# A layer with linear attention and a feed-forward branch on one core: chunks of 58 numbers laid out 64 apart

## The chip, the core and the metric

The kernel runs on one core of a Trainium2 chip. The core has five engines with instruction queues of their own: PE (TensorE, the matrix engine; its weight loads are listed as PEld), DVE (VectorE), ACT (ScalarE), POOL (GpSimd) and SP (SyncE, which here only issues DMAs). They meet through semaphores. Data lies in SBUF, matmul results in PSUM, which has eight banks of 512 fp32 numbers per partition. The metric is the device time of one execution in microseconds (us), taken as the median of several runs; beside it there is one profiled execution with a trace.

## The reference

One input x of 2048 tokens by 448 is normalised over its rows (layer norm), and two branches are added to it:

```python
def _A_ref(x, wqkv, w_phi, wo):                      # H = 16 heads, Dh = 28
    qkv = (x @ wqkv).reshape(B, S, 3, H, Dh) ...
    pq = einsum("bhsd,hdf->bhsf", q, w_phi)          # pk the same from k
    phi_q = concatenate([softmax(pq), softmax(-pq)], axis=-1)   # phi_k the same
    kv  = einsum("bhsf,bhsd->bhfd", phi_k, v)
    z   = einsum("bhsf->bhf", phi_k)
    num = einsum("bhqf,bhfd->bhqd", phi_q, kv)
    den = einsum("bhqf,bhf->bhq", phi_q, z)[..., None] + 1e-6
    return (num / den).transpose(...).reshape(B, S, D) @ wo

def _B_ref(x, w1, w2):                               # F = 1792
    return silu(x @ w1) @ w2

xn = _layernorm(x)
return x + _A_ref(xn, wqkv, w_phi, wo) + _B_ref(xn, w1, w2)
```

All inputs and the output are bf16. The attention is linear: kv and z are sums over all tokens, and no product of tokens with tokens is made.

## The kernel before

The 2048 tokens are 16 tiles of 128, mostly handled as pairs of tiles. The kernel first records operations (`P.op`, `P.dma`) with their reads and writes; a planner (`schedule`, L228) then gives every engine its order from estimated durations. For PE the order is fixed beforehand: the words of `PLAN` (L361) are taken one after the other and chained by `strict`. For the other engines the planner decides.

A word of `PLAN` has a phase, a kind, a number and, after `@`, the PSUM banks that it opens. The kinds: `F` is a block of the first feed-forward product (two column groups of 128 for 512 tokens), `v`, `k` and `q` are the projections of a pair of tiles, `K` is the kv product of two tiles, `M` joins and masks kv, `s` scales the query features of a pair, `U` is the attention product of a pair, `G` and `Y` are seven steps of the second feed-forward product of a pair, `W` is the output projection of a pair, `E` are the last feed-forward steps of the last two tiles. A product over 128 rows is made as two products over 64 rows that run side by side on the two halves of the matrix engine. Phase `a` has tile 0 of the pair on the lower and tile 1 on the upper rows, phase `b` the other way round, so each phase is half of the work of a block (`rows64`, L903). A half may begin only when the partner half that wrote the same bank from the other rows is done, and for that PE waits for its own semaphore.

The stretches that the change touches:

- `v_block` (L789) projects the values. Its evacuation (ACT, L542) writes them into `vaug` (L461), where each head has 28 values and a 1 (`DA` = 29); the ones give z. The ones are written by a clear on POOL (L1054).
- `kv` (L852) multiplies, for each tile and each chunk c of two heads, 128 columns of key features with the 58 numbers of the chunk, on both row halves. The results of a half gather in one bank, chunk c at columns 58c. These are 256 matmuls in 16 blocks of 8 chunks.
- `kvm` (L883): ACT copies one half out of PSUM, DVE adds the other (`kvsum`), and DVE multiplies by a mask that zeroes the cross terms of the two heads (`KVm`, L466, cleared on POOL, L1055).
- `att` (L956) multiplies the query features of a tile (stationary, in `phT`) with `KVm`, chunk by chunk, again 58 columns at 58c of a bank: 256 matmuls in 16 blocks.
- `normalise` (L967), after phase `b`: on DVE it adds epsilon to the denominators, takes the reciprocal and multiplies, into `o_sb`; SP issues one transposing DMA per tile (`dma_t`, L623) into `oT_sb`, which `wo_pair` (L984) reads. `o_sb` and `oT_sb` lie in the same memory as `vaug`, which is no longer needed then.
- After the last part of a pair, `finish_pair` (L1010) adds the other addend on DVE (L1001) and ACT issues the output DMA (L1003).

The query features come from `phi_q` (POOL, L874), behind the row sums (DVE, L837) and reciprocals (L838) of the exponents that ACT makes, and go through transposing DMAs on SP as well.

Before the change a chunk of the values starts at element 58c of its tile's row of 464 bf16 numbers, so at byte 116c, and a chunk of results at byte 232c of its bank.

Of the kernel before, what the change touches and what calls it, by code (L numbers as in the profile page):

```python
# [6 lines left out]
BF16 = mybir.dt.bfloat16  # L7
F32 = mybir.dt.float32
# [355 lines left out]
aF23@2 bF21 ak14@6 bF23 bY0 g0@1 bk14 bY0 aF13@0 aF19@2 bF13 aF24@6 aF20@4 bF19 bF20 bF24 ak10@0 g1@3 bk10 K0 K6 K4 aq4@2  # L364
K12 aq8@4 bq4 K8 K2 s4 aq0@0 bq8 aq6@2 K14 bq0 bq6 bY1@45 K10 M aY1 aq2@2 aF26@0 s6 bq2 bF26 bY1 aG3@23 aY1 aU2@67 s8 aF15@0
bU2 s0 bF15 aF16@4 bG3 bF16 aU4@01 aq12@6 bU4 bq12 aU3@45 bG3 bU3 s2 aq10@0 aG3 bq10 aq14@6 aW2@45 aG2 s10 bq14 aU0@01 bG2
bG2 aG4@67 bU0 bW4 bW2 bG4 s12 aG2 aW3 s14 aU1@01 bW3 aG4 aW4 bU1 bG4 bG5@23 aG6@41 aU5@50 aU6@67 bU5 aG5 bG6 aU7@05 bG6 bU6
aG6 bG5 bU7 aG5 aW0@67 bW5 bW0 aW5 aW6 aW1@05 aG7@672 aW7 bW6 bW1 bG7 bW7 E14 E15"""


def bass_parallel_sum__linear_kernel_hedgehog__dense_activation_silu__prompt_kernel(
# [19 lines left out]
    KS = (0, 128, 256, D - 128)  # L391
    CC = 8
    DA = DH + 1
    EPS_LN = 1e-5
    EPS_DEN = 1e-6
    NYT = 4
# [11 lines left out]
    with es:  # L408
        def sb(name, shape, dt):
            return es.enter_context(nc.sbuf_tensor(name, shape, dt))  # L410
# [32 lines left out]
        def ph_slots(n, w=1):  # L443
            at = n * CC * 128 + (SHIFT if n >= NT - 2 else 0)
            return flat[:, at:at + w * CC * 128].rearrange("p (t c j) -> p t c j", t=w, c=CC)
# [12 lines left out]
            c = t % 2 * EW  # L458
            return ek_pairs(t - t % 2, t - t % 2 + 2)[:, 0, c:c + w * EW].rearrange("p (n c) -> p n c", n=w)

        vaug = sb("vaug", [128, NT, H, DA], BF16)  # L461
        vflat = vaug[:].rearrange("p t h e -> p (t h e)")
        o_sb = vflat[:, 0:NO * 512].rearrange("p (n c) -> p n c", n=NO)
        oT_sb = vflat[:, NO * 512:(NO + NQ) * 512].rearrange("p (n g c) -> p n g c", n=NQ, g=G)
        kvsum = sb("kvsum", [KP, CC * 2 * DA], F32)
        KVm = sb("KVm", [128, CC, 2, DA], BF16)  # L466
        ident = sb("ident", [128, 128], BF16)
        ones_bf = sb("ones_bf", [128, 128], BF16)
        ones4 = sb("ones4", [128, 4], F32)
# [45 lines left out]
        def pe_mms(mms, name, dur=None, keys_w=(), mode=128):  # L515
            def fn(e):
                r = None
                for dst, lhsT, rhs, st, sp in mms:
                    r = e.matmul(dst, lhsT, rhs, start=st, stop=sp, skip_group_check=True)  # L519
# [28 lines left out]
        def memset(dst, v, n, name, eng="pool"):  # L548
            P.op(eng, d_pool(n, 0.5), lambda e: e.memset(dst, v), writes=[dst], name=name)  # L549
# [239 lines left out]
        def v_block(t, b0):  # L789
            fns = pair_block(b0, D, lambda i, kt, r: xnT[r, t + i, kt, :],  # L790
                             lambda i, kt, r: wv_sb[r, kt, :], "v")

            def evac():
                src = psum[:, b0 * 512:(b0 + 2) * 512].rearrange("p (i c) -> p i c", i=2)[:, :, 0:D].rearrange("p i (h d) -> p i h d", h=H)
                dst = vaug[:, t:t + 2, :, 0:DH]
                act(dst, src, ACTF.Identity, 896, f"v_ev{t}")

            return *fns, evac
# [53 lines left out]
        def kv(ts):  # L852
            def rows_k(t, c, r):
                at = t % 2 * EW + c * KP
                return ek_pairs(t - t % 2, t - t % 2 + 2)[r, 0, at:at + 128]

            P.cur_slack = 250.0
            pe_mms([(banks[KVB - i][:, c * 2 * DA:(c + 1) * 2 * DA], rows_k(t, c, r),
                     vaug[r, t, 2 * c:2 * c + 2, :].rearrange("p h c -> p (h c)"),
                     t == 0 and c == 0, t == NT - 1) for t in ts for c in range(CC) for i, r in enumerate((LOW, HIGH))],  # L860
                   "kv_mm", dur=CC * 29.0 * len(ts), keys_w=["kvbank"], mode=64)
            P.cur_slack = 0.0

        def slot(t):
            n = q_order.index(t)
            return n + 14 if n < 2 else n + 6 if n < 8 else n - 8
# [14 lines left out]
                      (1250.0, 2450.0)[w - 1], "phqT", (1250.0, 2000.0)[w - 1])  # L881

        def kvm():  # L883
            lo, hi = (banks[KVB - i][0:KP, 0:2 * DA * CC] for i in range(2))
            P.op("act", d_act(464), lambda e: e.activation(kvsum[:], hi, ACTF.Identity), reads=[hi], writes=[kvsum[:]], name="kvhi")
            P.op("dve", d_dve(464), lambda e: e.tensor_tensor(kvsum[:], lo, kvsum[:], ALU.add), reads=[lo, kvsum[:]], writes=[kvsum[:]], name="kvsum")
            src = kvsum[:].rearrange("p (c j e) -> p c j e", c=CC, j=2)
            P.op("dve", d_dve(464), lambda e: e.tensor_tensor(
                KVm[0:KP], src, mask2[:, None, :, None].broadcast_to([KP, CC, 2, DA]), ALU.mult),
                reads=[src, mask2[:]], writes=[KVm[0:KP]], name="kvm")  # L890


        early = {int(w[2]) for w in PLAN.split() if w[1:2] == "Y"}
# [62 lines left out]
        def att(p, turned, bs):  # L956
            both = []
            for side in range(2):
                i = side ^ turned
                both.append([(bs[i], slice(c * 2 * DA, (c + 1) * 2 * DA), ph_slots(slot(2 * p + i))[LO_HI[side], 0, c, :],  # L960
                              KVm[LO_HI[side], c, :, :].rearrange("p j e -> p (j e)")) for c in range(CC)])
            rows64(*both, "U_mm", CC * 31.2, 400.0, turned)
            if turned:
                for i in range(2):
                    normalise(2 * p + i, banks[bs[i]])

        def normalise(t, ub):  # L967
# [4 lines left out]
            U3 = ub[:, 0:H * DA].rearrange("p (h e) -> p h e", e=DA)  # L972
            P.op("dve", 190, lambda e: e.tensor_scalar(den[:, uq, :], U3[:, :, DH], EPS_DEN, None, ALU.add),
                 reads=[U3[:, :, DH]], writes=[den[:, uq, :]], name="den")
# [4 lines left out]
            o3 = o_sb[:, oq, off:off + D].rearrange("p (h d) -> p h d", d=DH)  # L979
            P.op("dve", 620, lambda e: e.tensor_tensor(o3, U3[:, :, 0:DH], rden[:, uq, :, None].broadcast_to([128, H, DH]), ALU.mult),  # L980
                 reads=[U3[:, :, 0:DH], rden[:, uq, :]], writes=[o3], name="o")
            dma_t(oT_sb[:, q, :, :], o_sb[:, oq, :], 620.0, "oT_dma")

        def wo_pair(p, turned, bs, last):  # L984
# [66 lines left out]
            ln_tile(t)  # L1051
        chain("ev3 bnst4".split())
        block_mask(mask2[:], 2 * DH, 2, KP)
        memset(vaug[:, :, :, DH], 1.0, 2150, "vaug1")  # L1054
        memset(KVm[:], 0.0, 464, "kvm0")  # L1055
        def k_block(t, b0):
            return proj_block(t, b0, True)

# [199 lines left out]
```

## Time and profile before

| | us |
|---|---|
| median of 3 runs | 145.98 |
| lowest and highest | 145.75, 146.19 |
| the profiled execution | 145.67 |
| its span, first to last instruction | 144.4 |
| PE busy in the span | 140.5 |
| DVE, ACT, POOL busy | 90.4, 79.7, 75.1 |

The page of the profile gives busy times per engine, the chain of work that ended last, and groups of instructions; further views are the timeline (instructions in order of time, equal ones merged: start, length, engine, line, operation, tiles, shape, count, and in brackets the idle time before it and who ended it), the view by tile, and windows (busy time per engine in a stretch). Every matmul is listed as `PE ... MATMUL` with "64*128 64x58" for 64 rows, 128 stationary columns and 58 moving columns. Matmuls are pipelined, so their listed durations overlap; the distance of the starts is the cost of a step. The mean granted clock of PE over the span is 1.00.

### The profile page before, as it was taken

The page shows a single profiled execution, that of the slowest core. Times are in us where ns is not written, and L with a number is a line of the kernel's source. Part 1 is how long each engine was busy: PE and PEld are TensorE (multiplying, and loading weights), DVE is VectorE, ACT ScalarE, POOL GpSimd, SP SyncE. Part 2 cuts the span into 40 slices and gives each one's busy share as a digit, 9 for nine tenths or more (in the row PEclk, how much of TensorE's full clock was granted, in tenths as well). Part 3 has the DMA queues.
Part 4 walks back from the last instruction along what each step waited for, and adds up shares of the span by engine and source line. Part 5 has one row for each costly group of instructions (what it writes and reads, how often), then busy time and mean ns, then how long its engine had stood idle before and what let it go on. Part 6 is the DMA issues. An engine that isn't in the chain of part 4 may idle for free.

```text
span 144.4 us, 4551 instructions
## 1 busy us (share of the span) xinstructions
PE 140.5 (97%) x1966; PEld 82.6 (57%) x1966; DVE 90.4 (63%) x195; ACT 79.7 (55%) x98; POOL 75.1 (52%) x95
## 2 busy tenths in 40 slices
PE   7799999999999999999999999999999999999994
PEld 7694445445444545476677655565555556555773
DVE  1969898700850079939049999957886564265163
ACT  4578775479996999889878948265440000000000
POOL 8807668620296009799935999991596500000000
DMA  3999989847960000000000068759689899524432
GB/s 90 330 346 299 278 180 91 155 88 166 354 182 5 0 2 5 0 0 5 0 5 5 5 124 161 120 108 184 97 166 164 203 197 181 108 53 97 130 127 64
DMA packets 44500, 17.59 MB, mean 122 GB/s; under 512 B 36912, under 2 KB 44096, under 8 KB 44480
## 3 DMA queue, kind: packets, MB, share of 16 engines
q1 hardware_dynamic: 41776, 15.22, 51.9%
q10 hardware_dynamic: 2576, 2.06, 5.4%
q8 instruction: 15, 0.25, 0.7%
q0 software_dynamic: 128, 0.03, 0.1%
q14 instruction: 5, 0.04, 0.1%
HBM read 6.57 MB, written 1.84 MB: 58 GB/s over the span
## 4 chain that ended last, share of the span: by engine, by line
PE 94%; DVE 2%; DMA 1%; issue 0%
PE psum L519 94%; DMA x_sb<-in_A_x_dram 1%; DVE st L701 1%; DVE RA L716 1%; PE psum L536 1%; DVE mv L702 0%; DVE x_sb L1001 0%; DVE rstd L707 0%
## 5 line engine op out<-in xcount | busy, mean ns | idle before, releaser
L519 PE MATMUL psum<-xnT,phT 64*128 64x512 bf16 (+1 forms) x428 | 46.8, 350 | 0.1
L519 PE MATMUL psum<-w_sb,hT 64*128 64x448 bf16 (+4 forms) x455 | 46.0, 341 | 0.0
L837 DVE TENSOR_REDUCE Rec<-Ek_sb 128x32 f32<-128x896 bf16 (+1 forms) x20 | 24.6, 1257 | 18.7 <-ACT Ek_sb L542 18.6
L542 ACT ACTIVATE hT<-psum 128x1024 bf16<-128x1024 f32 x28 | 27.6, 1024 | 11.0 <-PE psum L519 11.0
L519 PEld LDWEIGHTS psum<-w_sb,hT 64*128 64x128 bf16 (+1 forms) x455 | 23.6, 94 | 17.4 <-issue 0.2
L519 PEld LDWEIGHTS psum<-xnT,phT 64*128 64x128 bf16 (+1 forms) x428 | 22.5, 95 | 17.9 <-ACT vaug L542 0.6
L874 POOL TENSOR_TENSOR RA<-Ek_sb,Rec 128x896 bf16<-128x896 bf16 x16 | 27.0, 1721 | 5.8 <-DVE Rec L838 4.7
L519 PE MATMUL psum<-Wqk,xnT 64*128 64x432 bf16 x224 | 24.6, 343 | 0.0
L542 ACT ACTIVATE Ek_sb<-psum 128x864 bf16<-128x864 f32 x24 | 20.4, 915 | 7.2 <-PE psum L519 2.9
L847 POOL TENSOR_TENSOR Ek_sb<-Ek_sb,Rec 128x896 bf16<-128x896 bf16 x8 | 13.4, 1697 | 17.7 <-DVE Rec L838 17.7
L519 PEld LDWEIGHTS psum<-Wqk,xnT 64*128 64x128 bf16 x224 | 10.9, 94 | 8.1 <-ACT hT L542 0.4
L542 ACT ACT_TABLE_LOAD x11 | 14.1, 1283 | 2.1 <-POOL Wp L549 1.9
L847 POOL TENSOR_TENSOR phT<-phT,Rec 128x896 bf16<-128x896 bf16 x8 | 13.4, 1697 | 1.6 <-issue 0.9
L519 PE MATMUL psum<-wv,xnT 64*128 64x448 bf16 x112 | 12.4, 349 | 0.0
L1001 DVE TENSOR_TENSOR x_sb<-psum,x_sb 128x448 bf16<-128x448 f32 (+2 forms) x13 | 7.2, 584 | 7.5 <-PE psum L519 7.4
L701 DVE BATCH_NORM_STATS2 st<-x_sb 128x6 f32<-128x448 bf16 x16 | 9.7, 603 | 3.4 <-DMA x_sb<-in_A_x_dram 3.4
L519 PE MATMUL psum<-wo_sb,vaug 64*128 64x448 bf16 (+2 forms) x102 | 11.1, 338 | 0.1
L716 DVE TENSOR_SCALAR RA<-x_sb,mv,rstd 128x384 bf16<-128x384 bf16 (+4 forms) x29 | 9.1, 352 | 1.3 <-POOL rstd L712 1.2
L980 DVE TENSOR_TENSOR vaug<-psum,rden 128x448 bf16<-128x448 f32 x16 | 9.3, 620 | 0.0
L837 DVE TENSOR_REDUCE Rec<-phT 128x64 f32<-128x1792 bf16 x4 | 8.0, 1991 | 1.8 <-ACT phT L542 1.8
L838 DVE RECIPROCAL Rec<-Rec 128x32 f32<-128x32 f32 (+1 forms) x24 | 8.8, 396 | 0.2
L542 ACT ACTIVATE vaug<-psum 128x896 bf16<-128x896 f32 x8 | 7.3, 929 | 2.4 <-PE psum L519 2.4
(60 smaller groups left out, 106.3 us busy)
## 6 DMA issues: line engine op xcount, KB each, us to landing
out_dram<-x_sb ACTq DMA_DIRECT2D x15, 112.0 KB, 2.0
w_sb<-in_B_w_dram SPq DMA_DIRECT2D x1, 1568.0 KB, 7.8
x_sb<-in_A_x_dram SPq DMA_DIRECT2D x3, 448.0 KB, 6.3
wo_sb<-in_A_wo_dram SPq DMA_DIRECT2D x2, 336.0 KB, 7.4
phT<-in_B_w_dram SPq DMA_DIRECT2D x1, 576.0 KB, 7.4
phT<-in_B_w_dram SPq DMA_DIRECT2D x1, 384.0 KB, 5.1
wv<-in_A_wqkv_dram SPq DMA_DIRECT2D x1, 336.0 KB, 7.6
phT<-in_B_w_dram ACTq DMA_DIRECT2D x1, 256.0 KB, 4.6
```

What stands on the lines that cost most here:

```text
L519: r = e.matmul(dst, lhsT, rhs, start=st, stop=sp, skip_group_check=True)
L536: r = e.transpose(dst, src, ident[:])
L542: P.op("act", d_act(n), lambda e: e.activation(dst, src, func, scale=scale), reads=[src], writes=[dst], table=table, name=name, **keys)
L701: P.op("dve", 590, lambda e: e.bn_stats(st6[:, t, :], xs), reads=[xs], writes=[st6[:, t, :]], name=f"bnst{t}", okeys_w=["ln"])
L716: P.op("dve", dur, lambda e: e.tensor_scalar(dst, x_sb[:, t, c0:c1], mv[:, t, 0:1], rstd[:, t:t + 1], ALU.subtract, ALU.mult), reads=[xs, ...
L837: P.op("dve", 50 + 967 * n, lambda e: e.tensor_reduce(R2, E4, AXL.X, ALU.add), reads=[E4], writes=[R2], name=f"Ssum_{tag}")
L838: P.op("dve", 135 + 210 * n, lambda e: e.reciprocal(R2, R2), reads=[R2], writes=[R2], name="Rrec")
L847: P.op("pool", 1700, lambda e: e.tensor_tensor(E3, E3, Rk[:, :, None].broadcast_to([128, 32, DH]), ALU.mult), reads=[E3, Rk], writes=[E3], ...
L874: P.op("pool", 1700, lambda e: e.tensor_tensor(dst, Eq, Rq.rearrange("p (c j) -> p c j", c=CC)[:, :, :, None].broadcast_to([128, CC, 4, DH ...
L980: P.op("dve", 620, lambda e: e.tensor_tensor(o3, U3[:, :, 0:DH], rden[:, uq, :, None].broadcast_to([128, H, DH]), ALU.mult), reads=[U3[:, ...
L1001: P.op("dve", d_dve(cs.stop - cs.start), lambda e: e.tensor_tensor(res[:, cs], ob, addend[:, cs], ALU.add), reads=[ob, addend[:, cs]], wri ...
```

## The change

Values, masked kv and the results of both products get a pitch of 64 numbers per chunk (`CP`), of which the first 58 (`CW`) are used. The order of PE changes in three places: `K12` goes ahead of `aq4`, `bG5` ahead of `aG6`, and `bW6` ahead of `aG7` and `aW7`. The number of matmuls and their columns stay as they are. The planner's costs of the two products are set to other values. As the planner orders them, nothing but these three places changes on PE; SP, ACT and DVE keep their order, and on POOL four of eight small clears after the first kv products change places.

```diff
-aF23@2 ... ak10@0 g1@3 bk10 K0 K6 K4 aq4@2
-K12 aq8@4 bq4 K8 K2 s4 ...
+aF23@2 ... ak10@0 g1@3 bk10 K0 K6 K4 K12
+aq4@2 aq8@4 bq4 K8 K2 s4 ...
-... aU7@05 bG6 bU6
-aG6 bG5 bU7 aG5 aW0@67 bW5 bW0 aW5 aW6 aW1@05 aG7@672 aW7 bW6 bW1 bG7 bW7 E14 E15
+aU7@05 bG6 bU6 bG5 aG6 bU7 aG5 aW0@67 bW5 bW0 aW5 aW6 aW1@05 bW6 aG7@672 aW7 bW1 bG7 bW7 E14 E15
...
+    CW, CP = 2 * DA, 64
...
-        vaug = sb("vaug", [128, NT, H, DA], BF16)
-        vflat = vaug[:].rearrange("p t h e -> p (t h e)")
+        vaug = sb("vaug", [128, NT, CC, CP], BF16)
+        vflat = vaug[:].rearrange("p t c x -> p (t c x)")
+
+        def by_head(ap):
+            return ap[:, :, 0:CW].rearrange("p c (j e) -> p c j e", j=2)
...
-        kvsum = sb("kvsum", [KP, CC * 2 * DA], F32)
-        KVm = sb("KVm", [128, CC, 2, DA], BF16)
+        kvsum = sb("kvsum", [KP, CC, CW], F32)
+        KVm = sb("KVm", [128, CC, CP], BF16)
...
-                dst = vaug[:, t:t + 2, :, 0:DH]
+                dst = vaug[:, t:t + 2, :, 0:CW].rearrange("p i c (j e) -> p i c j e", j=2)[:, :, :, :, 0:DH]
...
-            pe_mms([(banks[KVB - i][:, c * 2 * DA:(c + 1) * 2 * DA], rows_k(t, c, r),
-                     vaug[r, t, 2 * c:2 * c + 2, :].rearrange("p h c -> p (h c)"),
+            pe_mms([(banks[KVB - i][:, c * CP:c * CP + CW], rows_k(t, c, r),
+                     vaug[r, t, c, 0:CW],
                      t == 0 and c == 0, t == NT - 1) for t in ts for c in range(CC) for i, r in enumerate((LOW, HIGH))],
-                   "kv_mm", dur=CC * 29.0 * len(ts), keys_w=["kvbank"], mode=64)
+                   "kv_mm", dur=CC * 26.5 * len(ts), keys_w=["kvbank"], mode=64)
...
-            lo, hi = (banks[KVB - i][0:KP, 0:2 * DA * CC] for i in range(2))
+            lo, hi = (banks[KVB - i][0:KP, 0:CC * CP].rearrange("p (c x) -> p c x", c=CC)[:, :, 0:CW] for i in range(2))
...
-                both.append([(bs[i], slice(c * 2 * DA, (c + 1) * 2 * DA), ph_slots(slot(2 * p + i))[LO_HI[side], 0, c, :],
-                              KVm[LO_HI[side], c, :, :].rearrange("p j e -> p (j e)")) for c in range(CC)])
-            rows64(*both, "U_mm", CC * 31.2, 400.0, turned)
+                both.append([(bs[i], slice(c * CP, c * CP + CW), ph_slots(slot(2 * p + i))[LO_HI[side], 0, c, :],
+                              KVm[LO_HI[side], c, 0:CW]) for c in range(CC)])
+            rows64(*both, "U_mm", CC * 27.5, 400.0, turned)
...
-            P.op("dve", 620, lambda e: e.tensor_tensor(o3, U3[:, :, 0:DH], rden[:, uq, :, None].broadcast_to([128, H, DH]), ALU.mult),
+            P.op("dve", 620, lambda e: e.tensor_tensor(o4, U4[:, :, :, 0:DH], rden4[:, :, :, None].broadcast_to([128, CC, 2, DH]), ALU.mult),
...
-        memset(vaug[:, :, :, DH], 1.0, 2150, "vaug1")
-        memset(KVm[:], 0.0, 464, "kvm0")
+        memset(vaug[:, :, :, 0:CW].rearrange("p t c (j e) -> p (t c) j e", j=2)[:, :, :, DH], 1.0, 2150, "vaug1")
+        memset(KVm[:], 0.0, 512, "kvm0")
```

More of the change, by code (lines that the diff above doesn't have):

```diff
@@ L363 @@
 bF17 bv14 aF18@4 bF14 aF27@6 ak4@2 bF27 bF18 bk4 ak6@0 av6@6 ak8@4 bv6 bk8 bk6 ak12@2 aF25@6 bk12 bF25 aY0@45 aY0 aF21@0
[L364 to L368, printed above, removed]
+aF23@2 bF21 ak14@6 bF23 bY0 g0@1 bk14 bY0 aF13@0 aF19@2 bF13 aF24@6 aF20@4 bF19 bF20 bF24 ak10@0 g1@3 bk10 K0 K6 K4 K12
+aq4@2 aq8@4 bq4 K8 K2 s4 aq0@0 bq8 aq6@2 K14 bq0 bq6 bY1@45 K10 M aY1 aq2@2 aF26@0 s6 bq2 bF26 bY1 aG3@23 aY1 aU2@67 s8
+aF15@0 bU2 s0 bF15 aF16@4 bG3 bF16 aU4@01 aq12@6 bU4 bq12 aU3@45 bG3 bU3 s2 aq10@0 aG3 bq10 aq14@6 aW2@45 aG2 s10 bq14
+aU0@01 bG2 bG2 aG4@67 bU0 bW4 bW2 bG4 s12 aG2 aW3 s14 aU1@01 bW3 aG4 aW4 bU1 bG4 bG5@23 aG6@41 aU5@50 aU6@67 bU5 aG5 bG6
+aU7@05 bG6 bU6 bG5 aG6 bU7 aG5 aW0@67 bW5 bW0 aW5 aW6 aW1@05 bW6 aG7@672 aW7 bW1 bG7 bW7 E14 E15"""
 def bass_parallel_sum__linear_kernel_hedgehog__dense_activation_silu__prompt_kernel(
@@ L793, in evac @@
             def evac():
-                src = psum[:, b0 * 512:(b0 + 2) * 512].rearrange("p (i c) -> p i c", i=2)[:, :, 0:D].rearrange("p i (h d) -> p i h d", h=H)
-                dst = vaug[:, t:t + 2, :, 0:DH]
+                src = psum[:, b0 * 512:(b0 + 2) * 512].rearrange("p (i c) -> p i c", i=2)[:, :, 0:D].rearrange("p i (c j d) -> p i c j d", c=CC, j=2)
+                dst = vaug[:, t:t + 2, :, 0:CW].rearrange("p i c (j e) -> p i c j e", j=2)[:, :, :, :, 0:DH]
                 act(dst, src, ACTF.Identity, 896, f"v_ev{t}")
@@ L883, in kvm @@
         def kvm():
-            lo, hi = (banks[KVB - i][0:KP, 0:2 * DA * CC] for i in range(2))
+            lo, hi = (banks[KVB - i][0:KP, 0:CC * CP].rearrange("p (c x) -> p c x", c=CC)[:, :, 0:CW] for i in range(2))
             P.op("act", d_act(464), lambda e: e.activation(kvsum[:], hi, ACTF.Identity), reads=[hi], writes=[kvsum[:]], name="kvhi")
             P.op("dve", d_dve(464), lambda e: e.tensor_tensor(kvsum[:], lo, kvsum[:], ALU.add), reads=[lo, kvsum[:]], writes=[kvsum[:]], name="kvsum")
-            src = kvsum[:].rearrange("p (c j e) -> p c j e", c=CC, j=2)
+            src = kvsum[:].rearrange("p c (j e) -> p c j e", j=2)
+            dst = by_head(KVm[0:KP])
             P.op("dve", d_dve(464), lambda e: e.tensor_tensor(
-                KVm[0:KP], src, mask2[:, None, :, None].broadcast_to([KP, CC, 2, DA]), ALU.mult),
-                reads=[src, mask2[:]], writes=[KVm[0:KP]], name="kvm")
+                dst, src, mask2[:, None, :, None].broadcast_to([KP, CC, 2, DA]), ALU.mult),
+                reads=[src, mask2[:]], writes=[dst], name="kvm")
         early = {int(w[2]) for w in PLAN.split() if w[1:2] == "Y"}
@@ L971, in normalise @@
             u_cnt[0] += 1
-            U3 = ub[:, 0:H * DA].rearrange("p (h e) -> p h e", e=DA)
-            P.op("dve", 190, lambda e: e.tensor_scalar(den[:, uq, :], U3[:, :, DH], EPS_DEN, None, ALU.add),
-                 reads=[U3[:, :, DH]], writes=[den[:, uq, :]], name="den")
+            U4 = by_head(ub[:, 0:CC * CP].rearrange("p (c x) -> p c x", c=CC))
+            den4, rden4 = (x[:, uq, :].rearrange("p (c j) -> p c j", j=2) for x in (den, rden))
+            P.op("dve", 190, lambda e: e.tensor_scalar(den4, U4[:, :, :, DH], EPS_DEN, None, ALU.add),
+                 reads=[U4[:, :, :, DH]], writes=[den[:, uq, :]], name="den")
             P.op("dve", 250, lambda e: e.reciprocal(rden[:, uq, :], den[:, uq, :]),
@@ L978, in normalise @@
             off = 64 * (n % 2)
-            o3 = o_sb[:, oq, off:off + D].rearrange("p (h d) -> p h d", d=DH)
-            P.op("dve", 620, lambda e: e.tensor_tensor(o3, U3[:, :, 0:DH], rden[:, uq, :, None].broadcast_to([128, H, DH]), ALU.mult),
-                 reads=[U3[:, :, 0:DH], rden[:, uq, :]], writes=[o3], name="o")
+            o4 = o_sb[:, oq, off:off + D].rearrange("p (c j d) -> p c j d", j=2, d=DH)
+            P.op("dve", 620, lambda e: e.tensor_tensor(o4, U4[:, :, :, 0:DH], rden4[:, :, :, None].broadcast_to([128, CC, 2, DH]), ALU.mult),
+                 reads=[U4[:, :, :, 0:DH], rden[:, uq, :]], writes=[o4], name="o")
             dma_t(oT_sb[:, q, :, :], o_sb[:, oq, :], 620.0, "oT_dma")
```

## The prediction

> **What bounds the kernel now.** I read the page first, then the chain of waits, then the timeline of the stretches that the change touches.
>
> ```profile
> span 144.4 us, 4551 instructions
> PE 140.5 (97%) x1966; PEld 82.6 (57%) x1966; DVE 90.4 (63%) x195; ACT 79.7 (55%) x98; POOL 75.1 (52%) x95
> ...
> PE 94%; DVE 2%; DMA 1%; issue 0%
> ```
>
> PE is busy for 97% of the span and makes up 94% of the chain that ended last. So a nanosecond saved on PE is a nanosecond of the end, unless PE then runs into something that does not come earlier with it. Two things therefore decide: what one step of the two changed products costs, and which waits stand close behind PE. The two products are 256 matmuls each, and this is the view by tile (instruction, count, then min/median/max of one in ns):
>
> ```profile
> L519 PE MATMUL psum<-KVm,phT x256: 184/187/195, 90.3 to 128.6; 64*128 64x58 bf16 x128
> L519 PE MATMUL psum<-vaug,Ek_sb x128: 184/187/188, 72.1 to 76.7; 64*128 64x58 bf16 x128
> L519 PE MATMUL psum<-vaug,phT x128: 184/187/188, 74.0 to 82.2; 64*128 64x58 bf16 x128
> ```
>
> A duration here holds the pipeline's depth; what counts is the distance from one start to the next. Two matmuls, one on each half of the rows, start together, so the unit is the pair, eight pairs (chunks 0 to 7) to a block. From the timeline of PE (start, length, count):
>
> ```profile
> 72.11 1.54 PE L519 MATMUL psum<-vaug,Ek_sb 64*128 64x58 bf16 x96
> 73.48 0.35 PE L519 MATMUL psum<-Wqk,xnT 64*128 64x432 bf16 x2
> ...
> 120.66 0.86 PE L519 MATMUL psum<-KVm,phT 64*128 64x58 bf16 x48
> 121.35 0.35 PE L519 MATMUL psum<-w_sb,hT 64*128 64x448 bf16 x2
> ```
>
> 48 pairs of the kv product take 73.48 - 72.11 = 1.37 us, 28.5 ns each; 24 pairs of the attention product take 0.69 us, 28.7 ns each. The mean hides two kinds: the minimum of 184 against the median of 187 says that a minority is 3 ns quicker. In the single starts these are always chunk 4, and chunk 0 where a block follows a block of its own kind: two of eight. With two at a and six at a + 3 a mean of 28.5 gives a = 26.3 and 29.3 ns. Chunk c of a row starts at 116c bytes; 0 and 464 alone are multiples of 16.
>
> **The change, part by part.** *The chunk pitch.* With 64 numbers to a chunk every chunk starts at a multiple of 128 bytes in SBUF and of 256 bytes in PSUM, so all eight should step as chunk 4 does. Both layouts change at once, so it does not matter whether the reading or the writing side makes the 3 ns. But the fast step shows in this product only between slow ones; that it can be kept up has to be read elsewhere. The weight fold has 56 columns at 112 bytes, a multiple of 16 at every chunk:
>
> ```profile
> 23.92 0.19 PE L519 MATMUL psum<-BD,wT 64*128 64x56 bf16 x1
> ...
> 24.13 0.38 PE L519 MATMUL psum<-xnT,phT 64*128 64x512 bf16 x2
> ```
>
> Eight fold pairs in 0.21 us, 26.2 ns each, one after the other without a slow one. So six pairs of a block lose 3 ns: 18 ns a block, over 16 kv and 16 attention blocks 32 x 18 = 0.58 us, of it 0.29 in each stage. The bounds: by the fold step unchanged (26.2 x 8 = 0.21 us against 0.228 and 0.230) 0.61; by the fold step scaled to 58 columns (27.1) 0.38; below nothing is excluded, since no column is added.
>
> The Trainium skill, TensorE: Matmul & The Clock Gate, section Back-to-back issue gap, gives a warm start-to-start of columns / 2.4 + 2.5 ns, an estimate of 26.7 ns for 58 columns; 32 blocks at that step would win 0.50 us in place of 0.58. The trace agrees for chunks 0 and 4 and not for the other six.
>
> *Waits that the shorter blocks uncover.* First, PE's wait for its own earlier half. Where a half-block waits for its partner on the other rows with only one attention block between, the block's length is the cover:
>
> ```profile
> 86.30 4.15 PE L519 MATMUL psum<-w_sb,hT 64*128 64x448 bf16 x42
> 90.27 0.40 PE L519 MATMUL psum<-KVm,phT 64*128 64x58 bf16 x16
> 90.50 0.82 PE L519 MATMUL psum<-xnT,phT 64*128 64x512 bf16 x6
> 91.14 0.41 PE L519 MATMUL psum<-KVm,phT 64*128 64x58 bf16 x16
> 91.39 0.39 PE L519 MATMUL psum<-xnT,phT 64*128 64x512 bf16 x2
> ```
>
> The block at 90.27 takes 0.23 us, the one at 91.14 takes 0.25: behind it stands the second half of an F block, which waits about 20 ns already. Such places in the new order are bF15, bq12, bW3 and bU5. The first gives back its 18 ns, the rest up to that: between 0 and 0.07 us, and I take 0.05. The swap of bG5 and aG6 puts 1.3 us between bG6 and aG6, where otherwise only a U block stood, so there nothing is lost; it moves 14 matmuls past 14 equal ones.
>
> Second, the masked matrix KVm, which the first attention block needs at 90.27. DVE is busy without a gap before it, and the chain does not begin with PE:
>
> ```profile
> 72.11 1.19 DVE L694 TENSOR_TENSOR Wqk<-psum,last_q 128x108 bf16<-128x108 f32 x3 [3.50 <-ACT last_q L542]
> 75.13 2.02 DVE L837 TENSOR_REDUCE Rec<-phT 128x64 f32<-128x1792 bf16 x1 [1.83 <-ACT phT L542]
> 77.19 0.55 DVE L838 RECIPROCAL Rec<-Rec 128x64 f32<-128x64 f32 x1
> 77.79 2.08 DVE L837 TENSOR_REDUCE Rec<-Ek_sb 128x32 f32<-128x896 bf16 x2
> 79.79 0.55 DVE L838 RECIPROCAL Rec<-Rec 128x32 f32<-128x32 f32 x2
> ...
> 88.95 1.07 DVE L888 TENSOR_TENSOR KVm<-kvsum,mask 112x464 bf16<-112x464 f32 x1
> ...
> 75.98 1.71 ACT L542 ACTIVATE Ek_sb<-psum 128x864 bf16<-128x864 f32 x2 [0.88 <-PE psum L519]
> ...
> 5.32 0.46 DVE RA L716
> 5.77 0.05 issue
> ```
>
> KVm is done at 90.02. The work ahead of the block, L837 to L888, has no idle time of its own in these rows. The shortest handover from DVE to PE that the chain of waits shows is 0.05 us, so PE may start at 90.07, 0.20 before it does. It will come 0.29 earlier, at 89.98. Part of that is made good: the reduce at 77.79 follows ACT's exponent that ends at 77.69 and that waits for PE (bq4). Eight kv blocks, K12's two among them, stand ahead of bq4, so it comes 0.14 earlier, and DVE can follow by 0.13, until its own reciprocal (done 77.74) holds it. Then PE may start at 89.94. So a stall between 0 and 0.09 us, and I take 0.05. K12 ahead of aq4 moves 32 matmuls past 6. aq4, at 73.48, needs the folded query weights that DVE ends at 73.30; six shorter blocks would bring it 0.11 sooner, close to that. With K12 first it comes 0.42 later instead, at no cost.
>
> *bW6 ahead of aG7 and aW7.* Here the trace of before has PE's one real stop after the head:
>
> ```profile
> 128.67 1.49 PE L519 MATMUL psum<-w_sb,hT 64*128 64x448 bf16 x14
> 130.00 0.73 PE L519 MATMUL psum<-wo_sb,vaug 64*128 64x448 bf16 x6
> ...
> 134.16 1.50 PE L519 MATMUL psum<-w_sb,hT 64*128 64x448 bf16 x21
> 135.72 0.46 PEld L519 LDWEIGHTS psum<-wo_sb,vaug 64*128 64x128 bf16 x8 [0.31 <-issue]
> 135.75 0.75 PE L519 MATMUL psum<-wo_sb,vaug 64*128 64x448 bf16 x9
> ```
>
> aG7 streams as many columns as the seven steps at 128.67, which take 1.33 us; so aW7 could start at 134.16 + 1.33 = 135.49 and starts at 135.75, 0.26 late. "issue" names no engine. It is the transposed output of the last pair, two DMAs on SP's queue (L624), of which one lands late:
>
> ```profile
> L624 SPq DMA_TRANSPOSE vaug<-vaug x4: 1196/1207/1217, 127.2 to 131.4; - x4
> ...
> DMA to landing us min/median/max: 2.4/2.5/4.3
> ...
> 133.30:134.00 0.70, 0.70 (x12) 0.33 (x10) 0.70 (x2) 0.00 (x0) 0.00 (x0) 1.00 0.46 153
> 134.00:135.25 1.25, 1.25 (x22) 0.99 (x19) 0.32 (x1) 0.00 (x0) 0.00 (x0) 1.00 0.14 22
> 135.25:135.65 0.40, 0.40 (x8) 0.16 (x2) 0.00 (x0) 0.00 (x0) 0.00 (x0) 1.00 0.78 262
> ```
>
> Of the four transposes from 127.2 on the median lands after 2.5 us, one after 4.3. With the last, issued at 131.4, that makes 135.7, when PE goes on. From 134.00 to 135.25 the queues move 22 GB/s, then 262 (the last two numbers of a row are DMA share and GB/s). Why they pause no row says. The new order puts bW6, 6 matmuls in three steps of 0.19, 0.57 us, between: aW7 asks 0.57 later, counted from the U7 block that feeds the chain. 0.57 is over 0.26, so the stop goes: 0.26 us won. Were the landing tied to the clock and not to U7, aW7, due at 135.49 - 0.48 + 0.57 = 135.58, would still be 0.17 late instead of 0.26: 0.09 won. bW6's own inputs are pair 6's transposes, which aW6 at 132.65 already uses. It releases pair 6's two evacuations (L1001) and output DMAs on ACT's queue about 2 us sooner, into a DVE that sits idle there. No DMA changes place on SP.
>
> *The rest, at nothing.* V evacuation (eight ACT instructions of 929 ns), the normalise group, kvsum and KVm get one level more in their access patterns and the same element counts. The rows nearest for DVE are a four-level subtraction and a plain add:
>
> ```profile
> L694 DVE TENSOR_TENSOR Wqk<-psum,last_k 128x432 bf16<-128x432 f32 x4 | 2.2, 601 | 0.8 <-ACT last_k L542 0.8
> ...
> L949 DVE TENSOR_TENSOR Y_sb<-psum,x_sb 128x448 f32<-128x448 f32 x4 | 2.3, 620 | 0.9 <-PE psum L519 0.9
> ```
>
> 601 ns for 432 elements and 620 for 448: levels cost nothing there. The clear of KVm grows from 464 to 512 elements, about 0.06 us on POOL at 3 us; what it delays, the fold's weights, is ready on POOL at 15.6 for a fold that starts at 23.92.
>
> **The sum.** -0.58 + 0.05 + 0.05 - 0.26 = -0.74 us. The profiled execution took 145.67 us, 144.4 of it span and 1.3 around it: 144.93, with a span near 143.7. The median of the three runs, 145.98, lies 0.31 above the profiled one, so I add that: 145.2 us.
>
> **The rivals.** *The step stays (no change).* The chunk's place in the run, not its address, could set the 3 ns: chunks 0 and 4 are also every fourth pair. Then only the stop at aW7 goes, -0.26: 145.7. For it: the period of four. Against it: eight fold pairs at 26.2 ns, where no period shows. The Trainium skill, SBUF — State Buffer, section Door 1: The DMA port swizzle, speaks of 16-byte lines with a price for each new line; 116 bytes touch eight lines from any of the starts 0, 4, 8 and 12 past a line, so by counting lines all chunks would cost the same. The trace disagrees with the count (184 against 187 ns), though the quick ones are those that start on a line.
>
> *The kv half is lost.* PE waits for KVm as long as it came earlier, 0.29 us, if DVE's chain does not move and the handover is as long as 0.25 us (that of before, 90.02 to 90.27). Then -0.74 + 0.24 = -0.50: 145.5. Against it: the 42 matmuls before 90.27 take 3.97 us, 0.19 a step, as everywhere (1.33 for seven), so PE did not stop there and that handover was no wait.
>
> *Slower: DVE pays for the extra level.* If a pattern with one level more ran at half speed, KVm would take 1.07 us longer (PE stops 1.07 at 89.98) and the last pair's two normalise products, 620 ns each, would land 1.24 later, of which bW6's spare 0.31 covers a part: 0.93 more. -0.74 + 1.07 + 0.93 = +1.3: 147.2. It decides from about 45% more per instruction, where 0.48 and 0.25 eat the whole gain. Against it: the 601 and 620 above.
>
> **How the numbers follow.** Forecast 0.68, step stays 0.13, kv half lost 0.11, DVE slower 0.08. About 0.3%, 0.44 us, is what can be told from no change here: faster means under 145.54. The forecast lies 0.3 under that line; its own range, from the bounds (step 0.38 to 0.61, waits 0 to 0.16, stop 0.1 to 0.26) and the scatter of the three runs, is 144.9 to 145.7; so a little of it counts as same, and a little over half of the kv rival as faster: faster 0.70, same 0.22, slower 0.08. The range takes in the first two rivals: 144.8 to 145.8.
>
> **What would show it.** By tile, the 58-column matmuls show a median of 184 instead of 187; the eight kv blocks ahead of aq4 take 8 x 0.21 = 1.7 us, an attention block 0.21. PEld has no stop of 0.3 us ahead of aW7. A PE gap at the first attention block, with KVm just ended, would show the second rival; KVm over 1.5 us or normalise over 0.9 the third. The prediction is wrong if the median is above 145.6, or if the steps stay at 28.5.

## The result and the profile after

| | us |
|---|---|
| before, median of 22 runs on the same chip | 146.03 |
| after, median of 22 runs | 145.35 |
| ratio after to before | 0.9957, interval 0.9937 to 0.9978 |
| the profiled execution after, its span | 145.35, 144.1 |

The changed kernel is faster by 0.4%, between 0.2 and 0.6%. Two profiled executions below, order_alone and kvm_psum, began some 2 us later and are shifted by that from there on; so lengths of stretches are compared here, and not spans.

First the page of the kernel after, its span and its busy times:

```profile
span 144.1 us, 4551 instructions
...
PE 141.0 (98%) x1966; PEld 82.7 (57%) x1966; DVE 90.6 (63%) x195; ACT 79.8 (55%) x98; POOL 75.3 (52%) x95
...
PE 95%; DVE 2%; DMA 1%; issue 0%
```

The engines do the same work; PE is still 95% of the chain. The view by tile of the kernel after (count, then min/median/max of one in ns):

```profile
L524 PE MATMUL psum<-KVm,phT x256: 185/185/198, 90.4 to 128.6; 64*128 64x58 bf16 x128
...
L524 PE MATMUL psum<-vaug,Ek_sb x128: 185/185/187, 72.4 to 76.8; 64*128 64x58 bf16 x128
L524 PE MATMUL psum<-vaug,phT x128: 185/185/187, 73.7 to 82.2; 64*128 64x58 bf16 x128
```

The median of 187 has become 185, and the minimum equals the median: there is one kind of matmul now instead of two. The timeline of PE in the kernel after, in the stretches that were shown of before:

```profile
72.41 1.46 PE L524 MATMUL psum<-vaug,Ek_sb 64*128 64x58 bf16 x96
73.69 0.60 PE L524 MATMUL psum<-vaug,phT 64*128 64x58 bf16 x32
74.11 0.72 PE L524 MATMUL psum<-Wqk,xnT 64*128 64x432 bf16 x6
...
86.37 4.15 PE L524 MATMUL psum<-w_sb,hT 64*128 64x448 bf16 x42
90.37 0.39 PE L524 MATMUL psum<-KVm,phT 64*128 64x58 bf16 x16
90.59 0.81 PE L524 MATMUL psum<-xnT,phT 64*128 64x512 bf16 x6
91.24 0.38 PE L524 MATMUL psum<-KVm,phT 64*128 64x58 bf16 x16
91.47 0.60 PE L524 MATMUL psum<-xnT,phT 64*128 64x512 bf16 x4
...
120.68 0.83 PE L524 MATMUL psum<-KVm,phT 64*128 64x58 bf16 x48
121.35 0.92 PE L524 MATMUL psum<-w_sb,hT 64*128 64x448 bf16 x8
...
128.40 0.38 PE L524 MATMUL psum<-KVm,phT 64*128 64x58 bf16 x16
128.61 1.49 PE L524 MATMUL psum<-w_sb,hT 64*128 64x448 bf16 x14
...
134.66 1.50 PE L524 MATMUL psum<-w_sb,hT 64*128 64x448 bf16 x21
135.99 0.76 PE L524 MATMUL psum<-wo_sb,vaug 64*128 64x448 bf16 x9
```

The eight kv blocks that now stand ahead of aq4 take 74.11 - 72.41 = 1.70 us, 26.6 ns a pair, where six of before took 1.37, 28.5 ns a pair. The three attention blocks at 120.68 take 0.67 instead of 0.69. aW7 starts at 135.99, 1.33 behind 134.66, which is what aG7 lasts: no stop. From the single starts of these rows, summed over the 16 blocks of each product, kv falls from 3648 to 3419 ns and attention from 3703 to 3543.

So the time between the first kv product and the end can be put together in stretches, each from the rows of the two profiles:

| stretch | before, us | after, us | change |
|---|---|---|---|
| first kv product to first attention block (72.11 to 90.27; 72.41 to 90.37) | 18.16 | 17.96 | -0.20 |
| first to last attention matmul (starts) | 38.38 | 38.22 | -0.16 |
| last attention matmul to last matmul of the output projection (starts) | 10.84 | 10.57 | -0.27 |
| from there to the end | 4.94 | 4.95 | +0.01 |

That is -0.62 us. Ahead of the first kv product the profile after is 0.30 longer (72.41 against 72.11), which is why its span is only 0.3 shorter. The other profiles of the two kernels have 72.23 (before) and 72.17 and 72.36 (after): it belongs to the single execution. So does part of the -0.62: from the first kv product to the end the two profiles of before have 72.32 and 72.14 us, the three of after 71.70, 71.91 and 71.74, so that the difference is between 0.23 and 0.62 by which two are compared. That the first pair agrees with the medians (146.03 - 145.35 = 0.68) so well is partly chance.

### The profile page after: what moved, and what is told of

It reads as the page before. It is cut to its first block, busy times and chain, and to the rows that moved or that the text cites. A ratio compares the mean times of both kernels' runs of the same rounds, so it can differ in the third digit from the quotient of the medians.

```text
span 144.1 us, 4551 instructions
## 1 busy us (share of the span) xinstructions
PE 141.0 (98%) x1966; PEld 82.7 (57%) x1966; DVE 90.6 (63%) x195; ACT 79.8 (55%) x98; POOL 75.3 (52%) x95
## 4 chain that ended last, share of the span: by engine, by line
PE 95%; DVE 2%; DMA 1%; issue 0%
PE psum L524 94%; DMA x_sb<-in_A_x_dram 1%; PE psum L541 1%; DVE st L706 1%; DVE RA L721 1%; DVE mv L707 0%; DVE x_sb L1008 0%; DVE rstd L712 0%
```

## The experiments

Twelve kernels ran, in batches that each share runs of the kernel before. All of them compute everything.

**Which part of the change does it.** Four kernels split the change. layout_alone has the new pitch and the old order; order_alone has the old layout and the new order; sbuf_only and psum_only have the new order and the pitch on one side only, either where the moving rows are read or where results are written.

```diff
 # sbuf_only: results dense again
-banks[KVB - i][:, c * CP:c * CP + CW]
+banks[KVB - i][:, c * CW:c * CW + CW]
...
-both.append([(bs[i], slice(c * CP, c * CP + CW), ...
+both.append([(bs[i], slice(c * CW, c * CW + CW), ...
 # psum_only: values and masked kv dense again
-vaug = sb("vaug", [128, NT, CC, CP], BF16)
+vaug = sb("vaug", [128, NT, CC, CW], BF16)
...
-KVm = sb("KVm", [128, CC, CP], BF16)
+KVm = sb("KVm", [128, CC, CW], BF16)
```

> The pitch of 64 with the old order of PE. Theory (the step and the stop at aW7 are two separate gains): the 58-column steps are 26.6 ns as in the changed kernel, but the stop ahead of aW7 stays or grows, from 0.26 to some 0.3 us, and one or two halves wait for their partner (aG6 behind bU6) or for the query weights (aq4), some 0.1 us: 0.2 to 0.35 us below the kernel before. Rival (the gain is nearly all in the step): 0.5 us or more below.

> The new order of PE with the old layout of 58. Theory: the steps stay at 28.5 ns, the stop ahead of aW7 is gone: 0.2 to 0.3 us below the kernel before. Rival (the late transpose moves with the order, so that aW7 stops again): no more than 0.1 us below.

> The changed kernel with the pitch of 64 in SBUF alone (values and masked kv); the results lie dense in PSUM, at 58. If reading the moving rows from a start off 16 bytes makes the 3 ns, the steps are 26.6 ns and the time that of the changed kernel. If writing the results off 32 bytes makes them, six of eight steps are back at 29 and it is 0.4 to 0.5 us slower than the changed kernel.

> The changed kernel with the pitch of 64 in PSUM alone; values and masked kv lie dense in SBUF, at 58. If the reading side makes the 3 ns, six of eight steps are back at 29 and it is 0.4 to 0.5 us slower than the changed kernel. If the writing side makes them, the steps are 26.6 ns. The masking instruction on DVE, 1182 ns in the changed kernel against 1066 before, goes back to 1066 if its pitched output made the difference.

| kernel | median, us | before, us | ratio, interval | sum of 16 kv blocks, ns | of 16 attention blocks, ns |
|---|---|---|---|---|---|
| layout_alone | 145.65 | 145.82 | 0.9988, 0.9969 to 1.0007 | 3468 | 3565 |
| order_alone | 145.82 | 145.82 | 1.0004, 0.9978 to 1.003 | 3644 | 3705 |
| sbuf_only | 145.30 | 145.82 | 0.9971, 0.9941 to 1.0001 | 3467 | 3542 |
| psum_only | 145.51 | 145.82 | 0.9992, 0.998 to 1.0004 | 3641 | 3699 |

The times alone separate little: order_alone was to lie 0.2 to 0.3 us below before and lies at it, layout_alone 0.2 to 0.35 and is 0.17 below, sbuf_only and psum_only were to lie 0.4 to 0.5 apart and are 0.21 apart. The traces separate all four. By tile, the kv product in psum_only and then in sbuf_only:

```profile
L524 PE MATMUL psum<-vaug,Ek_sb x128: 183/187/189, 72.2 to 76.7; 64*128 64x58 bf16 x128
```

```profile
L524 PE MATMUL psum<-vaug,Ek_sb x128: 183/185/198, 72.1 to 76.5; 64*128 64x58 bf16 x128
```

With only the results at a pitch the median stays 187 and the blocks stay at 3641 and 3699 ns; with only the values and KVm at a pitch it is 185, and the blocks are as short as with both. The 3 ns arise where the moving rows are read from SBUF. The maximum of 198 is one short stop in the kv stretch, to which the last section comes back. layout_alone shows in its single starts what the two small moves of the order are for: there PE stops 46 ns ahead of aq4, at 73.42, 0.10 behind the end of the folded query weights that aq4 needs (73.32), and the blocks at 125.28 and 128.17 last 13 ns longer, none of which is in after. That is 0.07 us.

**Is it the start address?** The prediction named a chunk's start on a multiple of 16 bytes as the cause. off2 is the changed kernel with all chunks moved by two elements within their 64, so that every one starts 4 bytes past such a multiple. w2_off2 does the same to the weights of the second feed-forward product, whose rows are 448 numbers, 896 bytes, one behind the other; no other line of the kernel changes.

```diff
 # off2
-    CW, CP = 2 * DA, 64
+    CW, CP, OFF = 2 * DA, 64, 2
...
-                     vaug[r, t, c, 0:CW],
+                     vaug[r, t, c, OFF:OFF + CW],
...
-                              KVm[LO_HI[side], c, 0:CW]) for c in range(CC)])
+                              KVm[LO_HI[side], c, OFF:OFF + CW]) for c in range(CC)])
 # w2_off2
-w2_sb = sb("w2_sb", [128, FT, D], BF16)
+w2_sb = sb("w2_sb", [128, FT * D + 2], BF16)[:, 2:2 + FT * D].rearrange("p (f d) -> p f d", f=FT)
```

> The changed kernel with values and masked kv moved by two elements inside each chunk's 64, so that all eight chunks start 4 bytes past a multiple of 16. If the start's address makes the 3 ns, all eight steps of a block are 29, chunks 0 and 4 too, about 20 ns more per block than in the changed kernel, 0.65 us over 32 blocks: as slow as the kernel before or 0.1 us slower. If the place of a chunk in the run (every fourth) makes them, or the pitch of 64, the steps stay at 26.6 and so does the time.

> The changed kernel with the second feed-forward weights, the moving rows of 448 columns, moved by two elements in SBUF, 4 bytes past a multiple of 16. If the price of such a start is one for each matmul, the seven steps of a G part take 7 x 3 = 20 ns more (1.33 to 1.35 us) and the kernel about 0.6 us more. If it is one for each stretch of columns, 3 ns for 58, a step of 448 takes 23 ns more, a part 0.16, and the kernel some 5 us more.

off2 took 145.37 against 145.87, ratio 0.9969 (0.9938 to 0.9999); by tile:

```profile
L525 PE MATMUL psum<-KVm,phT x256: 185/185/198, 90.4 to 128.7; 64*128 64x58 bf16 x128
```

No chunk starts on a multiple of 16, and all steps stay quick. The theory of the start address falls. w2_off2 took 145.67, ratio 0.9985 (0.9959 to 1.001), 0.39 us above after_again of the same batch where about 0.6 was expected; its timeline of PE, first and last attention block:

```profile
90.26 0.39 PE L524 MATMUL psum<-KVm,phT 64*128 64x58 bf16 x16
...
128.55 0.37 PE L524 MATMUL psum<-KVm,phT 64*128 64x58 bf16 x16
```

128.55 - 90.26 = 38.29 us, where the kernel after has 128.40 - 90.37 = 38.03. Between them stand 252 matmuls of the second feed-forward product, 126 pairs: 2.1 ns a pair. The mean distance of their starts rose from 189.2 to 191.5 ns, for 448 columns. In the single starts it is not spread evenly: the first step of each seven, behind other work, stays at 189.5, and the six that follow a neighbour in memory go from 189.2 to 191.8, 2.7 ns more. In kv the old layout loses 3648 - 3419 = 229 ns on 96 of 128 pairs, 2.4 ns each, for 58 columns. So the price is one per matmul and not one per column, and here the same 4 bytes that cost nothing in off2 do cost.

What tells the two apart is the neighbour. In off2 six unused elements lie between chunks; in w2_off2 each row begins where the one before ended, in the middle of a stretch of 16 bytes, and only the step without such a neighbour ahead of it stays quick. This gave a new theory: a matmul is slow when its moving rows begin in the 16-byte line of SBUF in which those of the matmul ahead of it ended. In the old layout chunk 4 begins at byte 464, a multiple of 16, chunk 0 behind the end of a row of 928 bytes, and the other six in their predecessor's last line. That rows touch is not enough: chunk 4 too begins where chunk 3 ended, and it is quick. Lines of 8 bytes do not fit: with them every other chunk would be quick (chunk 2 begins at 232, 29 times 8), and only one in four is.

**The neighbour, by itself.** dense_permuted is the sharpest form: the layout of before, byte for byte, and the new order of PE, but the eight chunks are multiplied in the order 0 2 4 6 1 3 5 7, so that no two neighbours in memory follow each other. pitch66 sets chunks 132 bytes apart: starts 0, 4, 8 and 12 bytes past a line, and no line shared.

```diff
 # dense_permuted, against order_alone
+    CORD = (0, 2, 4, 6, 1, 3, 5, 7)
...
-                     t == 0 and c == 0, t == NT - 1) for t in ts for c in range(CC) for i, r in enumerate((LOW, HIGH))],
+                     t == 0 and c == 0, t == NT - 1) for t in ts for c in CORD for i, r in enumerate((LOW, HIGH))],
...
-                              KVm[LO_HI[side], c, :, :].rearrange("p j e -> p (j e)")) for c in range(CC)])
+                              KVm[LO_HI[side], c, :, :].rearrange("p j e -> p (j e)")) for c in CORD])
 # pitch66, against sbuf_only
-    CW, CP = 2 * DA, 64
+    CW, CP = 2 * DA, 66
```

> Before's dense layout (chunks 116 bytes apart, no pitch) and the new order of PE; only the order in which the eight chunks of a block are multiplied changes, to 0 2 4 6 1 3 5 7, in both products. No two matmuls that follow each other on a half then share a 16-byte line of their moving rows. Shared line: all eight steps of a block at 26.6 ns, kv stretch to the first attention block 17.95 to 18.1 us instead of 18.16, first to last attention block 38.2 instead of 38.37, and KVm at 1.07 us (its output is dense again) instead of 1.18; the time equals after's or lies up to 0.1 us below it, ratio to before 0.994 to 0.998. Start address (the prediction's): chunks 0 and 4 alone are quick, the steps stay at 28.5 ns, 18.15 and 38.37 us, ratio as order_alone, 0.999 to 1.001.

> As sbuf_only (results dense in PSUM), but values and masked kv lie 66 numbers apart, 132 bytes, so that chunks start at 0, 4, 8 and 12 bytes past a 16-byte line and no two share a line. Shared line: all steps at 26.6 ns, 18.0 and 38.22 us as sbuf_only, ratio to before 0.996 to 0.999. Start address: chunks 0 and 4 at 26.6, the other six at 29.3 ns, 18.15 and 38.37 us.

> The changed kernel once more, to set the other two beside it on one chip: ratio to before 0.993 to 0.998, steps 26.6 ns, KVm 1.18 us.

dense_permuted, by tile and from the timeline of PE:

```profile
L520 PE MATMUL psum<-KVm,phT x256: 185/185/198, 90.2 to 128.4; 64*128 64x58 bf16 x128
```

```profile
72.23 1.46 PE L520 MATMUL psum<-vaug,Ek_sb 64*128 64x58 bf16 x96
73.51 0.60 PE L520 MATMUL psum<-vaug,phT 64*128 64x58 bf16 x32
73.94 0.91 PE L520 MATMUL psum<-Wqk,xnT 64*128 64x432 bf16 x8
```

73.94 - 72.23 = 1.71 us for 64 pairs: 26.7 ns, with the same addresses that cost 28.5 ns in the natural order. pitch66 has the median of 185 in both products too. Both fit the shared line and neither the address. pitch66 also rules out lines of 32 bytes: its gaps are 16 bytes, so that two or three of the seven borders inside a block would lie in one such line, and no step there is slow. In time dense_permuted has 145.32 against 145.81, ratio 0.9964 (0.9938 to 0.9991), beside 0.9972 (0.9947 to 0.9997) of after_third in the same batch: the reordering of a loop buys what the change buys with a new layout, and neither is shown to beat the other. pitch66 has 145.41, ratio 0.9979 (0.9946 to 1.0011), with a stop of 0.3 us in the kv stretch of its profile.

**What KVm waits for.** One part of these expectations missed. In after KVm's multiplication takes 1182 ns instead of 1066; psum_only, whose KVm is dense, had 1073, and so I put the difference down to the pitched output. But dense_permuted, also dense, has 1192. The rows that explain it are POOL's. The timelines of POOL in before, of POOL in after, and of DVE in after:

```profile
87.82 1.70 POOL L874 TENSOR_TENSOR RA<-Ek_sb,Rec 128x896 bf16<-128x896 bf16 x1
```

```profile
88.11 1.70 POOL L879 TENSOR_TENSOR RA<-Ek_sb,Rec 128x896 bf16<-128x896 bf16 x1
```

```profile
87.64 0.58 DVE L891 TENSOR_TENSOR kvsum<-psum,kvsum 112x464 f32<-112x464 f32 x1
88.14 1.07 DVE L842 TENSOR_REDUCE Rec<-Ek_sb 128x32 f32<-128x896 bf16 x1
89.13 1.18 DVE L894 TENSOR_TENSOR KVm<-kvsum,mask 112x464 bf16<-112x464 f32 x1
```

In before POOL's multiplication ends at 89.52 and KVm at 88.95 + 1.07 = 90.02; in after they end at 89.81 and 90.31. It is 0.50 us both times, and so in every profile of this study but that of the kernel below: 496 to 500 ns in thirteen of them. DVE starts KVm earlier, by the clock of the first kv product (16.84 us behind it in before, 16.72 in after), and KVm ends 17.9 behind it in both. The Trainium skill, SBUF — State Buffer, section Who interferes with whom, says that a DVE instruction with two inputs in SBUF and a GpSimd instruction that reads SBUF exclude each other, so that the later one waits; KVm reads kvsum and the mask, both in SBUF. kvm_psum tests it: dense_permuted with the sum of the halves left in PSUM, so that KVm reads one input from SBUF.

```diff
-e.tensor_tensor(kvsum[:], lo, kvsum[:], ALU.add)
+e.tensor_tensor(lo, lo, kvsum[:], ALU.add)
...
-            src = kvsum[:].rearrange("p (c j e) -> p c j e", c=CC, j=2)
+            src = lo.rearrange("p (c j e) -> p c j e", c=CC, j=2)
```

> As dense_permuted, but DVE writes the sum of the two kv halves back into PSUM and takes it from there for the mask, so that KVm's multiplication reads one tensor from SBUF (the mask) in place of two. In every trace so far KVm ended 0.50 us behind POOL's sixth multiplication of key or query features, 18.0 us after the first kv product, whatever PE did. Theory that KVm is held by POOL: KVm takes 0.5 to 0.65 us in place of 1.07 to 1.20 and ends near 17.4, POOL's next multiplication takes 1.70 instead of 2.10, PE waits no more ahead of the first attention block (17.92 to 17.98 from the first kv product to it) and the time falls by 0 to 0.1 us against dense_permuted. Rival, that the broadcast multiplication itself takes that long: KVm stays at 1.07 to 1.20 and POOL's next at 2.10.

Its timelines of DVE, and then of POOL:

```profile
89.47 0.62 DVE L887 TENSOR_TENSOR psum<-psum,kvsum 112x464 f32<-112x464 f32 x1
90.00 1.07 DVE L838 TENSOR_REDUCE Rec<-Ek_sb 128x32 f32<-128x896 bf16 x1
90.99 0.63 DVE L889 TENSOR_TENSOR KVm<-psum,mask 112x464 bf16<-112x464 f32 x1
```

```profile
89.95 1.69 POOL L875 TENSOR_TENSOR RA<-Ek_sb,Rec 128x896 bf16<-128x896 bf16 x1
```

KVm takes 0.63 us and is done at 91.62, while POOL's multiplication still runs until 91.64. POOL gains as well: by tile its 16 multiplications have a maximum of 2092 ns in after and of 1702 here.

```profile
L879 POOL TENSOR_TENSOR RA<-Ek_sb,Rec x16: 1692/1697/2092, 81.5 to 112.6; 128x896 bf16<-128x896 bf16 x16
```

```profile
L875 POOL TENSOR_TENSOR RA<-Ek_sb,Rec x16: 1690/1697/1702, 83.3 to 114.9; 128x896 bf16<-128x896 bf16 x16
```

So the lengthening of KVm was a wait for POOL, shown by taking the second input away, and the statement holds here. In time kvm_psum has 145.29 against 145.65, ratio 0.9933 (0.9892 to 0.9974). This interval covers most of that of after (0.9937 to 0.9978), so no difference from after is shown; little was to be won, since PE lost next to nothing to KVm. It goes from the first kv product to the first attention block in 17.93 us instead of 17.96.

**Once more the same kernels.** before_again and after_again are before and after unchanged, to see what a second profile shows.

> The kernel before once more, under a name of its own: its ratio to itself shows what a comparison of this kind can tell, and its profile gives a second sample of the stop ahead of aW7. If the stop belongs to the program it is 0.2 to 0.3 us again; if it hangs on how the transfers fall in a run it lies between 0 and 0.3.

> The changed kernel once more. If the gain of the first comparison holds, the ratio is between 0.994 and 0.998; the profile should show the head (to the first kv product) within 0.1 us of the kernel before, if the 0.3 us by which it was longer in the first profile is a matter of the single run, and 0.3 us longer again if the change makes it.

before_again: 145.64, ratio 0.9988 (0.9967 to 1.001). after_again: 145.28, ratio 0.9954 (0.9933 to 0.9975). The timeline of PE ahead of aW7 in before_again, and then in layout_alone, which has the old order as well:

```profile
134.29 1.50 PE L519 MATMUL psum<-w_sb,hT 64*128 64x448 bf16 x21
135.69 0.72 PE L519 MATMUL psum<-wo_sb,vaug 64*128 64x448 bf16 x8
```

```profile
133.89 1.50 PE L524 MATMUL psum<-w_sb,hT 64*128 64x448 bf16 x21
135.27 0.75 PE L524 MATMUL psum<-wo_sb,vaug 64*128 64x448 bf16 x9
```

With 1.33 us for aG7 the stop is 0.07 and 0.05 us here, against 0.26 in the profile that the prediction used. The last transposing DMA is late in each of them; by tile before_again has

```profile
L624 SPq DMA_TRANSPOSE vaug<-vaug x5: 1197/1216/2172, 124.1 to 131.5; - x5
...
DMA to landing us min/median/max: 2.4/2.5/4.1
```

so 131.5 + 4.1 = 135.6, when PE, due at 134.29 + 1.33 = 135.62, has just come. In the profile of before it was 4.3 and PE was due at 135.49. In after the last landing takes 4.1 too, from 131.3 on, and aW7 is due at 135.99.

## Why the prediction was right, point by point

The forecast was 145.2 us, the median 145.35; 0.74 us was to be won, 0.63 (0.0043 times 146.03, interval 0.32 to 0.92) was. The direction and the four places were right, two of the terms were too large and one cause was wrong. That the total came so near is partly luck: the stretches above give -0.20 - 0.16 = -0.36 for everything but the stop, and with the stop, which lasted 0.05, 0.07 and 0.26 in the three profiles with the old order, between -0.41 and -0.62.

*The chunk pitch, -0.58.* Right that six of eight steps are 3 ns slower than the other two and that the pitch makes all eight alike; mis-sized, and with the wrong cause. The step came to 26.65 ns and not to the fold's 26.2: over 256 pairs 0.115 us less, so -0.23 in kv (3648 to 3419 ns) and -0.24 in attention before its own waits. The estimate of 26.7 ns from the Trainium skill's formula for the gap of a matmul taken alone (TensorE: Matmul & The Clock Gate, section Back-to-back issue gap) agrees with the measured step. The bound from the fold scaled to 58 columns, 27.1, lay on the other side; of the two ends I took the nearer row and not the nearer shape. "Chunks 0 and 4 alone are multiples of 16" described the pattern, but off2 and pitch66 show quick steps off the multiples, and dense_permuted shows quick steps at the old addresses: what decides is the line shared with the matmul ahead. The rival of the place in the run was nearer to this than the address was, since what decides is what stands ahead; that it would leave the time as it was did not follow, because the pitch takes the sharing away as well. In the fold no line is shared as long as its rows begin on a multiple of 16 bytes, 112 bytes being seven lines, so that row could not tell the two causes apart.

*PE waiting for its own half, +0.05.* Right in kind, somewhat low. In the single starts of after, a block that a half-block waits for lasts 227 to 229 ns instead of 215: at 91.24, 95.94, 108.80, 113.58, 116.47 and 120.90. That is about what a block lasted before, so at these places next to nothing was won. The block at 121.12, ahead of aG5, lasts 226 as well; its partner half was done long before, and what it waits for is open. The first had waited some 20 ns already; in all about 0.07 us was given back. The blocks at 108.80 and 116.47, ahead of bW4 and bG4, cost as much as the ones that were named and were missed. With 0.07 and 0.01 more in the first block, which waits for KVm, attention gives 0.16 us and not 0.24.

*KVm, +0.05.* Right in size, 0.03 to 0.04: the 42 matmuls ahead of the first attention block take 90.37 - 86.37 = 4.00 us instead of 3.97, and PE starts 0.06 behind KVm's end, near the shortest handover. The way there was another. DVE's chain followed by 0.12 us, as worked out, but KVm's end did not move, because it was held 0.50 behind POOL. The reason that the loss is small is the 0.26 of slack between KVm and PE in the old order, of which the change used 0.20. The rival "the kv half is lost" had the right picture, an end of KVm that does not move, and the wrong handover, 0.25 instead of 0.06.

*bW6 ahead of aG7 and aW7, -0.26.* The mechanism was right: the stop is gone in every profile with the new order but after_again, where the last transpose took longer to land and 0.08 was left. The size was read from one execution. Two more profiles with the old order have 0.07 and 0.05, and order_alone gives 1.0004, between 0.32 won and 0.44 lost. The profiles alone, by the stretch from the first kv product to the end, put the new order at 0.08 to 0.26 (72.05 in order_alone against 72.14 and 72.32). What it is worth in the median stays open; "all of 0.26" is not shown. The step that failed is that a length between two late events was taken from a single profile as if it were a duration.

*The rest, at nothing.* Right: the normalise product has 620 ns a piece before and after, the clears on POOL stay hidden. V's evacuation went from 929 to 948 ns on ACT, off the path. KVm's 1182 ns was no price of the access pattern.

## What to carry to other kernels

Where a stream of short matmuls reads rows that lie end to end, look at the distances of the starts and not at the mean: a period in them points to the layout, and changing only the order of the loop shows whether it is the address or the neighbour. A wait of 0.2 us between two engines in one profile is worth a second profile before it enters a sum. When an instruction on DVE with two inputs in SBUF takes twice the time that its size suggests, compare its end with the end of what POOL is doing before blaming its shape.

## What the hardware showed that was not expected

A matmul whose moving rows begin in the 16-byte line in which those of the one ahead ended costs 2.4 to 2.7 ns more, with 58 columns (kv, before against after) as with 448 (w2_off2 against after). The Trainium skill, SBUF — State Buffer, section Door 1: The DMA port swizzle, counts a price for each new line; by that count off2, dense_permuted and before would have stepped alike, with eight lines to a chunk in all of them, and they do not. Why a shared line costs anything no run here shows.

In seven of the nine profiles with quick steps and the new order PE stops once inside the kv stretch, always behind the first pair of the twelfth block, 4.2 us behind the first kv product, by 0.02 to 0.3 us, with no wait for another engine in the listing; in the two with slow steps and the new order it does not. In after_again and off2 it is 0.15 us, in pitch66 0.3 (that block takes 520 ns instead of 213). after itself is one of the two without it, so its share of the kernel's median is not known. It may be that instructions arrive too late for the faster stream; that was not tried, and the loss stays unexplained.
